# A scan and a mixture of adapters on one core: stores of four chunks, five transfers under way, new orders

## The chip, the cores and the metric

The kernel runs on one core of a Trainium2 chip. The metric is the device time of one execution in microseconds; where several runs are told of, it is their median.

## The reference

Two inputs `a` and `b` of shape (8, 6400, 128) in float32 go through a first-order recurrence along the sequence, and its output through a mixture of eight adapters of rank 16, of which each row uses its two best.

```python
for t in range(S):                      # S = 6400, h of shape (8, 128)
    h = a[:, t] * h + b[:, t]
    out[:, t] = h
x = out.reshape(51200, 128)
logits = x @ w_gate                     # (51200, 8)
topk = np.argpartition(-logits, 2, axis=1)[:, :2]
w = softmax of the two logits
delta[rows of expert e] += w * ((x @ A[e]) @ B[e])      # A: 128x16, B: 16x128
return x + delta
```

## The kernel before

The 51,200 rows are cut into 100 **chunks** of 512 rows, of four **blocks** of 128 rows each. A chunk goes through these steps, whose names are those of the orders below:

- `la`, `lb` (L396): SyncE loads `a` and `b` in tiles `a_tm` and `b_tm`, two chunks (512 KB) at a time; the first four chunks come singly, and ScalarE issues one of their loads. From chunk 4 on a partition takes eight rows, 4 KB, that follow each other in memory. There are `NL` = 6 places for each input.
- `A`, `B`, `P` (L417): TensorE transposes `a` into `pA` and `b` into `pB`; `P` holds `b` of a chunk and `a` of the next, woven. `fi` (L446) are transposes to fill time.
- `ae` (L435): ScalarE copies `pA` to `a_st`.
- `sc` (L482): VectorE runs the scan along 512 columns and writes `xT` in float16. Every 6,400 rows it starts anew, which makes two scans of a chunk in some cases. `xT` holds `NX` = 24 chunks.
- `Z` (L500), `ze` (L506): TensorE multiplies a unit of mostly six blocks of x with the adapters' down-projection and the gate's weights; ScalarE copies the result to `zl`, which holds `NZ` = 120 blocks.
- `g1` to `g8`, `gx`, `w1`: the gate's weights for a group of up to four units, on VectorE and GpSimd, with a sigmoid (`w1`) on ScalarE.
- `mu` (L569): GpSimd, sometimes VectorE, multiplies `zl` with the weights to `zw`.
- `T` (L578), `te` (L300): transposes of `zw` and their copy to `zwT`, by VectorE or ScalarE.
- `D` (L588, L589): for each block the product with the identity brings x back, and the one with `B` adds the delta, in `pO`.
- `oe` (L300): a copy to `outt`, mostly by ScalarE. It holds `NO` = 72 blocks, 18 chunks.
- `st` (L631): SyncE stores finished chunks, 48 times two chunks and 4 times one. A store's chunks lie in one **tile** of x in which a partition holds rows that follow each other in memory (8 rows, 4 KB, for two chunks). `Z` picks its blocks across that tile, so it waits for the scan of the tile's last chunk. The store of chunks 68 and 69 goes in two DMAs, of 124 and of 4 partitions (`SPLIT`).

Each engine executes its instructions in an order that is written out in `ORDER`. Each step lists the steps that it depends on, and `waits()` makes of these the semaphore waits, leaving out those that another wait implies. A load waits for the transposes of what stood in its place before; a store waits for the copies of its chunks; a copy to `outt` waits for the store of what stood there. An engine that waits holds up everything behind it in its order; SyncE issues loads and stores in one order. At the end SyncE waits for the landing of the stores.

Of the kernel before, what the change touches and what calls it, by code (L numbers as in the profile page):

```python
# [9 lines left out]

UNITS = [4] * 3 + [6] * 62 + [4] * 4
GROUPS = [1, 2] + [4] * 15 + [2, 1, 1, 1, 1]
STORES = [2] * 48 + [1] * 4
SPLIT = {68: [124, 4]}
TOP8 = 4
WARM = 16
FILL = {k: 4 for k in range(7, 15)}
HEAD = 4
NL = 6
NA = 3  # L20
NX = 24
NZ = 120
NO = 72
NW = 4
NG = 8
NS = 16
TAIL_CHUNKS = 12
ORDER = {
# [16 lines left out]
    ),  # L45
    "act": (
# [16 lines left out]
    ),  # L63
    "dve": (
# [14 lines left out]
    ),  # L79
    "pool": (  # L80
# [8 lines left out]
    ),  # L89
# [9 lines left out]
    ),  # L99
}  # L100

# [26 lines left out]
        assert len(named) == len(self.ops)  # L128
        self.order = {e: [named[name] for name in ORDER[e].split()] for e in self.ENGINES}
        assert sum(len(o) for o in self.order.values()) == len(self.ops)  # L130
        for e in self.ENGINES:
            n = 0
            for op in self.order[e]:
# [597 lines left out]
```

## Time and profile before

| | |
|---|---|
| median of three runs | 201.57 us (201.27 to 201.87) |
| profiled execution | 201.01 us |
| its span, first to last instruction | 199.2 us |
| busy: PE, DVE, ACT, POOL | 185.2, 175.0, 176.9, 136.0 us |
| moved by DMA | 79.26 MB, mean 398 GB/s |
| granted TensorE clock | 0.994 |

PE is TensorE's matmul, PEld its weight load, DVE VectorE, ACT ScalarE, POOL GpSimd, SP SyncE. A `q` behind an engine's name is its sequencer, which issues DMAs and waits. L396 is line 396 of the kernel. The DMA share is the mean busy share of the core's sixteen DMA engines; it can go above 1 because packets overlap on an engine. "To landing" is the time from a DMA's issue until its semaphore tells of its end. Durations come from the one profiled execution.

### The profile page before, as it was taken

How to read it: one execution, taken by the hardware profiler on the slowest of the kernel's cores; microseconds unless marked ns; L12 is line 12 of the kernel's file. 1: busy time of each engine (PE TensorE's matmuls, PEld its weight loads, DVE VectorE, ACT ScalarE, POOL GpSimd, SP SyncE). 2: the span in 40 equal slices, each digit the busy share in tenths (PEclk: the TensorE clock that was granted, in tenths of full speed). 3: DMA queues.
4: the chain of work that ended last, by engine and by line, in shares of the span. 5: the costliest groups of instructions: out<-in, count | busy, mean ns of one | idle time of the engine just before them, and what ended most of it. 6: DMA issues, size and time to landing. Idle time of an engine off the chain costs nothing.

```text
span 199.2 us, 7709 instructions
## 1 busy us (share of the span) xinstructions
PE 185.2 (93%) x3224; PEld 165.5 (83%) x3224; DVE 175.0 (88%) x291; ACT 176.9 (89%) x327; POOL 136.0 (68%) x168
## 2 busy tenths in 40 slices
PE   6899999999998979999999999999999999999990
PEld 6778888889987968899989989889988978878970
DVE  1599999989999879799999999999999899899980
ACT  2378699999988979899999999999999989999981
POOL 3210186878786657969989998796598978676520
PEclk9999999999999999999999999999999999999997
DMA  5999999999999999999999999999999999999796
GB/s 214 385 414 406 410 407 407 409 406 410 411 410 413 414 411 412 415 414 408 414 415 406 411 410 416 411 411 415 414 412 414 417 410 412 406 393 392 298 405 254
DMA packets 22921, 79.26 MB, mean 398 GB/s; under 512 B 2664, under 2 KB 2920, under 8 KB 22888
## 3 DMA queue, kind: packets, MB, share of 16 engines
q1 hardware_dynamic: 22312, 78.39, 98.1%
q8 instruction: 25, 0.41, 0.8%
q10 hardware_dynamic: 576, 0.40, 0.6%
q14 instruction: 8, 0.07, 0.1%
HBM read 52.56 MB, written 26.21 MB: 395 GB/s over the span
## 4 chain that ended last, share of the span: by engine, by line
PE 80%; ACT 5%; DMA 4%; issue 3%; SPq 2%; POOL 2%; DVE 1%; DVEq 0%
PE pB L417 23%; PE pO L588 13%; PE pZ L500 13%; PE pO L578 12%; PE pO L589 10%; PE pA L417 5%; DMA a_tm<-in_a_dram 4%; ACT outt L300 3%; PE pA L446 2%; SPq L396 2%; POOL zw L569 2%; ACT zwT L300 1%; ACT a_st L435 1%; ACT zl L506 1%; DVE xT L482 1%
## 5 line engine op out<-in xcount | busy, mean ns | idle before, releaser
L482 DVE TENSOR_TENSOR_SCAN xT<-a_st,xT,pB 128x512 f16<-128x512 f32 x96 | 120.4, 1254 | 6.6 <-PE pA L417 3.1
L569 POOL TENSOR_TENSOR zw<-zl,g 128x512 f16<-128x512 f32 x90 | 94.5, 1065 | 29.2 <-DVE g L554 23.2
L417 PE MATMUL pB<-ident_f,b_tm 64*128 64x64 f32 (+1 forms) x784 | 67.5, 229 | 1.2 <-issue 0.5
L417 PE MATMUL pA<-ident_f,a_tm 64*128 64x64 f32 (+1 forms) x784 | 67.8, 229 | 0.6 <-issue 0.4
L435 ACT COPY a_st<-pA 128x512 f32<-128x512 f32 x100 | 59.0, 613 | 7.9 <-PE pA L417 7.2
L417 PEld LDWEIGHTS pB<-ident_f,b_tm 64*128 64x128 f32 (+1 forms) x784 | 55.8, 139 | 10.9 <-issue 3.4
L506 ACT COPY zl<-pZ 128x816 f32<-128x816 f32 (+1 forms) x69 | 58.1, 842 | 1.7 <-PE pZ L500 1.6
L588 PE MATMUL pO<-ident_h,xT 128*128 128x128 f16 x368 | 55.2, 233 | 2.0 <-issue 1.8
L417 PEld LDWEIGHTS pA<-ident_f,a_tm 64*128 64x128 f32 (+1 forms) x784 | 56.0, 139 | 1.2 <-DMA a_tm<-in_a_dram 0.7
L300 ACT COPY outt<-pO 128x512 f32<-128x512 f32 x87 | 52.2, 609 | 4.6 <-PE pO L589 4.1
L589 PE MATMUL pO<-cst_h,zwT 128*128 128x128 f16 x368 | 53.0, 219 | 1.7 <-issue 1.7
L588 PEld LDWEIGHTS pO<-ident_h,xT 128*128 128x128 f16 x368 | 46.3, 144 | 4.9 <-issue 2.1
L589 PEld LDWEIGHTS pO<-cst_h,zwT 128*128 128x128 f16 x368 | 39.6, 108 | 1.8 <-issue 1.8
L500 PE MATMUL pZ<-cst_h,xT 128*128 128x136 f16 x400 | 37.8, 229 | 0.5 <-issue 0.4
L578 PE MATMUL pO<-ident_h,zw 128*128 128x128 f16 x368 | 35.5, 220 | 1.1 <-POOL zw L569 0.4
L500 PEld LDWEIGHTS pZ<-cst_h,xT 128*128 128x128 f16 x400 | 30.6, 145 | 1.5 <-DVE cst_h L324 0.2
L578 PEld LDWEIGHTS pO<-ident_h,zw 128*128 128x128 f16 x368 | 22.3, 97 | 5.5 <-POOL zw L569 1.3
L300 DVE COPY zwT<-pO 128x512 f16<-128x512 f16 x56 | 23.0, 414 | 3.5 <-PE pO L578 3.1
L300 ACT COPY zwT<-pO 128x512 f16<-128x512 f16 x36 | 21.4, 600 | 0.9 <-PE pO L578 0.8
L545 POOL TENSOR_TENSOR L<-L,k 128x192 f32<-128x192 f32 x14 | 8.8, 631 | 4.6 <-DVE L L543 4.0
L482 DVE TENSOR_TENSOR_SCAN xT<-a_st,pB 128x512 f16<-128x512 f32 (+1 forms) x8 | 7.5, 938 | 4.5 <-PE pB L417 4.4
L548 POOL TENSOR_TENSOR k<-k,L 128x192 f32<-128x192 f32 (+1 forms) x17 | 9.1, 535 | 2.5 <-DVE L L539 1.8
(56 smaller groups left out, 120.0 us busy)
## 6 DMA issues: line engine op xcount, KB each, us to landing
a_tm<-in_a_dram SPq DMA_DIRECT2D x48, 512.0 KB, 13.3
b_tm<-in_b_dram SPq DMA_DIRECT2D x48, 512.0 KB, 13.4
out_dram<-outt SPq DMA_DIRECT2D x47, 512.0 KB, 11.9
a_tm<-in_a_dram SPq DMA_DIRECT2D x4, 256.0 KB, 4.9
out_dram<-outt SPq DMA_DIRECT2D x4, 256.0 KB, 4.0
b_tm<-in_b_dram SPq DMA_DIRECT2D x3, 256.0 KB, 5.6
out_dram<-outt SPq DMA_DIRECT2D x1, 496.0 KB
b_tm<-in_b_dram ACTq DMA_DIRECT2D x1, 256.0 KB, 4.0
```

Source lines behind the costliest of these rows:

```text
L300: return e.copy(dst, src) if e is eng["act"] else e.tensor_copy(dst, src)
L417: last = e.transpose(*args)
L435: lambda e: e.copy(a_st[c % NA][:, :], pA[:, c % 2, :]))
L482: last = e.tensor_tensor_scan(out=x[:, s0:s1], data0=a_st[c % NA][:, s0:s1], data1=pB[:, c % 2, s0:s1], initial=init, op0=ALU.mult, op1=AL ...
L500: last = e.matmul(pZ[:, k // (n // 2), o : o + W], xblock(b0 + k), Awg_h)
L506: lambda e: e.copy(zl[:, zb : zb + n, :].rearrange("p (h k) w -> p h (k w)", h=2), pZ[:, :, 0 : n // 2 * W]))
L545: d3 = wide(5, [d3], lambda e: e.tensor_tensor(out=ll, in0=ll, in1=kk, op=ALU.add))
L548: d6 = wide(7, [d2, d5], lambda e: e.tensor_tensor(out=kk, in0=kk, in1=ll, op=ALU.add))
L569: lambda e: e.tensor_tensor(out=wv, in0=zv, in1=gv, op=ALU.mult))
L578: last = e.transpose(ptile[:, k * 128 : k * 128 + 128], zz[:, k, :], ident_h[:, :])
L588: e.matmul(dst, xblock(b0 + k), ident_h[:, :], start=True, stop=False)
L589: last = e.matmul(dst, zt[:, k * 128 : k * 128 + 128], B_h, start=False, stop=True)
```

## The change

- Stores take four chunks: two stores of two chunks, 23 of four, four of one. A partition's rows of a four-chunk store lie in one stretch of 8 KB. The tiles of x follow, so that `Z` waits for the scan of the last of four chunks.
- Four stores, those from chunk 20, 44, 68 and 84, go in five DMAs each, of 112, 4, 4, 4 and 4 partitions; the one split of before is gone.
- On SyncE each transfer also waits until the fifth before it in the order has landed. A store in parts counts as one.
- Five places for loads (6), 32 chunks of `xT` (24), 96 blocks of `zl` (120), 96 blocks of `outt` (72).
- New orders on all engines. The engine of some steps changes: 92 output copies are on ScalarE (95) and 8 on VectorE (5); 40 copies to `zwT` are on ScalarE (38) and 60 on VectorE (62); 11 `mu` on VectorE (10); among the gate's steps some go from one of VectorE and GpSimd to the other.

```diff
-STORES = [2] * 48 + [1] * 4
-SPLIT = {68: [124, 4]}
+STORES = [2,2]+[4]*23+[1]*4
+SPLIT = {c:[112,4,4,4,4] for c in (20,44,68,84)}
...
-NL = 6
+NL = 5
 NA = 3
-NX = 24
-NZ = 120
-NO = 72
+NX = 32
+NZ = 96
+NO = 96
...
+AHEAD = 5
 ORDER = {
     "pe": (
...
     "sp": (
-        "la0 lb1 la1 la3 lb2 la2 lb3 la4 lb4 la6 lb6 la8 lb8 la10 lb10 la12 lb12 la14 lb14 la16 lb16 la18 lb20 lb18 "
-        "la20 la24 la22 st0 lb22 la26 lb24 lb26 la28 la30 lb30 st2 lb28 lb34 la32 la34 lb32 lb36 la36 st6 st4 lb38 "
...
-        "st60 la98 st62 st72 st64 lb98 st66 st68 st78 st76 st70 st74 st82 st80 st86 st84 st90 st88 st92 st94 st96 "
-        "st97 st98 st99 "
+        "la0 la1 la2 lb1 la3 lb2 la4 lb3 lb4 la6 lb6 la8 lb8 la10 lb10 la12 lb12 lb14 la14 la16 lb18 lb16 la18 la20 "
+        "lb20 lb24 la22 st0 lb22 la24 la28 la26 lb26 lb28 st2 lb30 la30 la32 lb34 la36 lb32 la34 la38 lb36 st8 lb38 "
+        "la40 lb40 st12 la42 lb42 lb46 la44 lb44 lb48 la46 la48 st4 la50 lb52 lb50 la54 la52 st20 la56 lb54 la60 lb56 "
...
+        "lb92 la94 st52 lb94 la96 lb96 lb98 la98 st56 st60 st64 st76 st72 st68 st80 st84 st88 st92 st96 st97 st99 "
+        "st98 "
     ),
 }
...
         assert sum(len(o) for o in self.order.values()) == len(self.ops)
+        for before, op in zip(self.order["sp"], self.order["sp"][AHEAD:]):
+            op.deps = op.deps + [before]
```

More of the change, by code (lines that the diff above doesn't have):

```diff
@@ L12 @@
 GROUPS = [1, 2] + [4] * 15 + [2, 1, 1, 1, 1]
-STORES = [2] * 48 + [1] * 4
-SPLIT = {68: [124, 4]}
+STORES = [2,2]+[4]*23+[1]*4
+SPLIT = {c:[112,4,4,4,4] for c in (20,44,68,84)}
 TOP8 = 4
 WARM = 16
-FILL = {k: 4 for k in range(7, 15)}
+FILL = {k:4 for k in range(7,15)}
 HEAD = 4
-NL = 6
+NL = 5
 NA = 3
-NX = 24
-NZ = 120
-NO = 72
+NX = 32
+NZ = 96
+NO = 96
 NW = 4
```

111 rows, old and new, of the table ORDER are left out of this document.

## The prediction, made before the changed kernel ran

> **What bounds the kernel now.** I began with the slices of the page, because the change is about transfers, and then its queues and landing times.
>
> ```profile
> span 199.2 us, 7709 instructions
> PE 185.2 (93%) x3224; PEld 165.5 (83%) x3224; DVE 175.0 (88%) x291; ACT 176.9 (89%) x327; POOL 136.0 (68%) x168
> ...
> DMA  5999999999999999999999999999999999999796
> ...
> DMA packets 22921, 79.26 MB, mean 398 GB/s; under 512 B 2664, under 2 KB 2920, under 8 KB 22888
> ...
> q1 hardware_dynamic: 22312, 78.39, 98.1%
> q8 instruction: 25, 0.41, 0.8%
> ...
> a_tm<-in_a_dram SPq DMA_DIRECT2D x48, 512.0 KB, 13.3
> ...
> out_dram<-outt SPq DMA_DIRECT2D x47, 512.0 KB, 11.9
> ```
>
> The DMA digits are 9 from the second slice to the 37th. SyncE's queue q1 carries 78.39 MB and fills 98.1% of sixteen engines' span. A load of 512 KB lands 13.3 us after its issue. The next view cuts the span into stretches; its columns are busy time by engine with instruction counts, granted clock, DMA share, GB/s.
>
> ```profile
> 30.00:60.00 30.00, 28.64 (x543) 25.83 (x543) 28.32 (x37) 29.04 (x53) 23.71 (x28) 1.00 1.03 410
> 60.00:90.00 30.00, 27.49 (x510) 24.75 (x508) 26.22 (x40) 27.04 (x51) 21.64 (x26) 1.00 1.03 413
> 90.00:120.00 30.00, 29.85 (x560) 27.25 (x559) 29.15 (x40) 29.71 (x56) 27.85 (x35) 1.00 1.02 411
> 120.00:150.00 30.00, 29.48 (x554) 26.88 (x553) 28.57 (x44) 29.27 (x54) 23.45 (x28) 1.00 1.03 413
> 150.00:182.00 32.00, 30.39 (x526) 26.48 (x524) 29.44 (x55) 30.39 (x58) 25.97 (x29) 1.00 1.01 408
> 182.00:188.00 6.00, 5.93 (x96) 5.64 (x95) 6.00 (x24) 6.00 (x15) 2.59 (x4) 1.00 0.78 312
> 188.00:196.00 8.00, 5.96 (x89) 5.04 (x86) 5.10 (x23) 6.14 (x14) 2.12 (x3) 1.00 1.01 398
> ```
>
> The share is at or above 1.01 in every stretch from 30 to 182 us, at 408 to 413 GB/s. No engine is free either: ACT is busy for 29.7 of 30 us in one stretch. So two paces have to be compared. A chunk moves 256 KB of a, of b and of output, 786 KB, which at 412 GB/s is **1.91 us of transfers a chunk**. For the other pace I took the scans alone, stretch by stretch (busy time of DVE with the count, clock, share, GB/s):
>
> ```profile
> 30.00:60.00 30.00, 23.82 (x19) 1.00 1.03 410
> 60.00:90.00 30.00, 20.00 (x18) 1.00 1.03 413
> 90.00:120.00 30.00, 23.41 (x20) 1.00 1.02 411
> 120.00:150.00 30.00, 21.26 (x18) 1.00 1.03 413
> 150.00:180.00 30.00, 17.28 (x15) 1.00 1.02 408
> ```
>
> Between 30 and 150 us 75 scans run, some five of them second halves of a chunk where a batch begins: 70 chunks in 120 us, **1.71 us of computing a chunk**. From 150 to 180 there are 15 scans in 30 us, 2 us each. The engines run faster than the transfers for as long as loads issued ahead and free output places allow, and then fall back to the transfers' pace. The chain of waits on the page shows the opposite, 80% PE; but it follows the last releaser, and PE is kept supplied as long as loads are issued ahead of stores. The end confirms it:
>
> ```profile
> L396 SPq DMA_DIRECT2D b_tm<-in_b_dram x1: 445/445/445, 164.8 to 164.8; - x1
> ...
> DMA to landing us min/median/max: 13.3/13.3/13.3
> ```
>
> The last load is issued at 164.8 and lands at 178.1. In SyncE's order 33 stores of two chunks stand ahead of it, so 34 chunks, 8.9 MB, follow; at 412 GB/s that is 21.6 us, and the span ends 21.1 us later. The transfers are the bound to the last microsecond, and the sum is made on them.
>
> **The change part by part.**
>
> *Rows of 8 KB.* 23 stores of four chunks take the place of 46 stores of two. Their 92 chunks are 5,888 packets of 4 KB now and 2,944 of 8 KB then; bytes stay. Counted with their parts, 53 store transfers become 45, at 16 completion packets each: 128 fewer. Together 3,072 packets go from q1. What a packet costs beside its bytes comes from two pairs of windows of the DMA view, of which each pair differs in the mean size:
>
> ```profile
> q1 hardware_dynamic: 4499, 16.39, 101.5%
> ...
> q1 hardware_dynamic: 1116, 2.98, 82.7%
> ...
> q1 hardware_dynamic: 695, 1.26, 88.7%
> ...
> q1 hardware_dynamic: 685, 2.49, 103.1%
> ```
>
> The first is 60 to 100 us: 1.015 x 16 engines x 40 us = 649.6 us for 4,499 packets and 16.39 MB. The second is 190 to 199.2 us: 121.7 us for 1,116 packets and 2.98 MB. Solved for a price per packet and one per MB they give **12 ns a packet** and 36.3 us a MB. The third and fourth, 4 to 8 us and 10 to 16 us, give 19 ns in the same way, but there the constants' small packets share the engines. I take 12, since that pair holds stores. The saving is 3,072 x 12 ns / 16 engines = **2.3 us**; 19 ns would make it 3.6, and a price of nothing 0. A loss is bounded by the one row with packets of 16 KB: q8's 25 take 0.8% of 3,187 us, 1.02 us each, 62 us a MB. I give that no weight for the size, because such a packet takes turns with q1's on its engine, which the share above 1 shows.
>
> The Trainium skill, "DMA: Bandwidth & Descriptors", section "Why small descriptors are slow", speaks for less: a fixed three cycles or so a packet, which at the 850 MHz of its bandwidth section is an estimated 3.5 ns. By it the saving would be 0.7 us, and the total about 201.5. The rows above say 12 to 19 ns, and I go by them.
>
> *Four stores in five parts.* Today one store goes in parts of 124 and 4 partitions; afterwards four go in 112, 4, 4, 4, 4. Their bytes are the same. SyncE issues 16 more DMAs, at 0.45 us (the row of the last load) 7 us of its time, beside waits of 78 us below. I cost it at 0, with both signs open. If small parts use fewer engines than a full one, those fall behind by twelve 8 KB rows in all, 12 x 310 ns = 3.7 us, unless they were ahead; today's 124-part, in rows of 4 KB, would do the like.
>
> *Five under way.* Each transfer on SyncE now also waits until the fifth before it has landed. Behind such a wait stands everything later on SyncE, loads and stores; PE, and through it ACT and DVE, wait for the loads.
>
> ```profile
> SPq L396 <- PE pA L417: 36.1, 26, 4.3
> SPq L631 <- ACT outt L300: 23.3, 13, 5.0
> ...
> SPq L631 <- ACT sd L549: 12.9, 4, 8.8
> SPq L670 <- DVE outt L300: 5.8, 1, 5.8
> ...
> DMA to landing us min/median/max: 3.1/3.9/4.3
> ```
>
> Of these the last row is of the loads issued in the first 2 us, 256 KB each: 3.1 us for one that finds nothing ahead. At 1.27 us for 512 KB, today's 13.3 us are ten transfers deep; afterwards there are five, 6.4 us. When one lands, four are left, 5.1 us of work, and the next one's first byte needs some 3.1 - 0.6 = 2.5 us, so nothing runs dry unless SyncE then stands for over 2.6 us. Today it stands up to 4.3, 5.0, 5.8 and 8.8 us. But it will reach each transfer later, by up to 13.3 - 6.4 = 6.9 us, in which the engines move on; one load place less (two chunks, 3.8 us) takes part of that back, and 3.1 us are left. All but the 8.8 then fall near or below 2.6. At the start the first five are issued by 3 us, and the sixth waits for the first, landed at 3.8 to 4 us, while four of 256 KB are still to come. I cost the gate at 0; without that cover it is 4 us, below.
>
> *More output places, and the orders.* 72 blocks become 96, xT goes from 24 chunks to 32, zl from 120 blocks to 96. In the new order 15 stores (56 chunks) precede the last load, now 33 (66 chunks): it lands 2.6 MB / 412 = 6.4 us earlier, and 1.2 us more by packets already saved, near 170.5. The transfers' total is not changed by that, but it gives the engines room at the end:
>
> ```profile
> 193.67 1.17 ACT L300 COPY outt<-pB 128x512 f32<-128x512 f32 x2 [0.23 <-PE pB L589]
> ...
> L300 ACT COPY outt<-pO 128x512 f32<-128x512 f32 x87 | 52.2, 609 | 4.6 <-PE pO L589 4.1
> ```
>
> Today the last copy ends at 194.8, 16.7 us after the last load. From 170.5 that gives 187.2, where stores would still have some 9 us to go. ACT does three output copies fewer, DVE three more, and two zwT copies go from DVE to ACT; both engines' sums move by under 2 us. Z of a unit now waits for the scan of the last of four chunks, not of two; PE's order still places another P and further steps between that P and the Z.
>
> *The coarse end.* A four-chunk store can't start before its fourth copy; the last of them waits two copies longer than one of two chunks, 2 x 0.61 = 1.2 us, or 0 if the queue holds work then. I take half, **0.6 us**.
>
> **Sum.** 199.2 - 2.3 + 0.6 = 197.5 us of span. With the 1.8 us around it (the profiled execution took 201.01 us) that is 199.3, and since the median of the runs, 201.57, is 0.56 above that execution, **199.8 us**.
>
> **The rivals.**
>
> *The gate starves the engines (slower).* Its place is SyncE's wait ahead of a load that is drawn forward (la60 goes before la58, lb46 before la44) and whose place must first be emptied. It decides once SyncE stands for more than 2.6 us with four under way. With 3.1 us gained, the two longest waits of today would leave 8.8 - 3.1 - 2.6 = 3.1 us and 5.8 - 3.1 - 2.6 = 0.1 us; if the later arrival gains only 2.7, 3.5 and 0.5, so 4 us: 199.8 + 4 = **203.8 us**. For it: the transfers have no slack, every idle microsecond of theirs is one of the total. Against it: the load waits, 36.1 us in 26 cases, are short (mean 1.4).
>
> *A row's size is worth nothing.* If the bytes alone set a packet's time, only the 0.6 us stays: 202.2, or 201.6 if the queue hides that too; **201.8 us**. Against it are both pairs of windows. The skill's three cycles belong here.
>
> *The engines become the bound.* With all five busy, the new orders may cost the engines their 0.2 us a chunk of lead. At 1.91 us a chunk nothing would be gained; 0.02 us a chunk worse is 2 us: **203.5 us**. Against it stand 75 scans in 120 us.
>
> *The end gains too.* From 182 to 188 us the share is 0.78: 0.23 x 6 = 1.4 us of idle engines because stores were not ready. If the earlier last load closes that, **198.4 us**.
>
> **How the numbers follow.** Forecast 0.50, end gains too 0.11, row size worthless 0.13, gate starves 0.18, engines bound 0.08. About 0.3%, 0.6 us, is what a measurement of this kernel can tell from no change. Faster: 0.50 + 0.11 = 0.61, and 0.01 of the worthless-rows case; within 0.3%: the rest of that, 0.12; slower: 0.26. The range goes from 198.2, the end's gain with a little of a 19 ns packet, to 202.8, half of the gate's price and the worthless rows; beyond it lie most of the gate's and half of the engines' case, under 2 in 10.
>
> **What would show it.** q1 should have some 3,070 packets fewer at 78.4 MB; the share should stay at or above 1.0 from 10 us on past 180; loads should land some 6 to 7 us after issue; the last load should land near 171. If the share sags below 0.95 in a middle stretch while SyncE waits for PE, the gate was mispriced. If the share holds and the GB/s don't rise above 412, the row size was. If PE, DVE or ACT runs on to within 4 us of the end with the last stores landing at once, the engines are the bound.

## The result, and the profile after

The changed kernel takes **208.18 us** (median of four runs, 207.12 to 212.88), the kernel before 201.42 us: a ratio of 1.0316, 95% interval 1.0248 to 1.0383. Runs more than 1.5% above the fastest of their kernel count in the medians given here but not in the ratios: it is the one of 212.88 us here, and one of four in the experiments without the gate, with parts of 16, with parts for the early stores and with the last split store whole. The forecast was 199.8 us with a range to 202.8. The kernel is 6.4 us slower where 1.8 us of gain were expected.

The page of the kernel after, with the rows that answer to those of before:

```profile
span 205.4 us, 7749 instructions
...
PE 185.8 (90%) x3224; PEld 165.4 (81%) x3224; DVE 176.1 (86%) x289; ACT 177.8 (87%) x327; POOL 135.0 (66%) x171
...
DMA  6999999999999999989999999999999999999796
GB/s 221 383 413 407 404 409 285 411 397 374 408 397 409 391 401 416 416 310 359 402 415 405 416 412 406 413 420 397 415 406 387 415 410 414 427 412 369 249 380 260
DMA packets 19682, 79.27 MB, mean 386 GB/s; under 512 B 2368, under 2 KB 2624, under 8 KB 16704
...
q1 hardware_dynamic: 19072, 78.39, 97.2%
...
a_tm<-in_a_dram SPq DMA_DIRECT2D x48, 512.0 KB, 6.7
b_tm<-in_b_dram SPq DMA_DIRECT2D x48, 512.0 KB, 7.4
```

The engines do the same work: PE 185.8 us for 185.2, ACT 177.8 for 176.9. The bytes of q1 are the same, its packets are 3,240 fewer (3,070 were expected), and loads land 6.7 and 7.4 us after issue, as expected of five under way. But the mean pace fell from 398 to 386 GB/s. The DMA digits hardly show it: below 9 stand only an 8 in the eighteenth slice, where before there was a 9, and the 7 in the thirty-eighth, which was there before. The GB/s row shows three holes: the seventh slice (285), the eighteenth and nineteenth (310, 359), and the thirty-eighth (249). By stretches (busy time by engine with counts, granted clock, DMA share, GB/s), the kernel after:

```profile
30.00:60.00 30.00, 28.28 (x528) 25.13 (x526) 27.66 (x35) 28.72 (x54) 21.46 (x26) 1.00 1.01 380
60.00:90.00 30.00, 29.59 (x562) 27.02 (x561) 28.63 (x43) 29.46 (x55) 23.26 (x30) 1.00 1.00 397
90.00:120.00 30.00, 27.35 (x512) 24.45 (x510) 26.80 (x38) 27.81 (x51) 23.88 (x28) 1.00 1.01 393
120.00:150.00 30.00, 29.90 (x561) 27.30 (x560) 28.46 (x46) 28.68 (x54) 26.27 (x33) 1.00 1.02 411
150.00:182.00 32.00, 29.80 (x522) 26.35 (x516) 28.18 (x46) 28.95 (x53) 24.48 (x30) 1.00 1.01 410
182.00:190.00 8.00, 7.75 (x111) 6.75 (x111) 7.94 (x28) 7.88 (x18) 4.16 (x4) 1.00 1.02 382
190.00:199.00 9.00, 6.97 (x102) 5.80 (x100) 6.75 (x26) 6.95 (x16) 2.57 (x6) 1.00 0.82 300
199.00:205.40 6.40, 0.00 (x0) 0.00 (x0) 0.00 (x0) 0.00 (x0) 0.00 (x0) 0.54 0.74 291
```

From 30 to 120 us the share is 1.00 to 1.01 where the kernel before has 1.02 to 1.03, and the pace is 380 to 397 GB/s where that one has 410 to 413. The share counts the time that packets take, however slowly they go: it fell by 1 to 3%, the pace by 4 to 7%. From 190 us on both fall. SyncE's waits in the kernel after (total, times, longest):

```profile
SPq L397 <- DMA b_tm<-in_b_dram: 33.6, 39, 1.9
SPq L397 <- DMA a_tm<-in_a_dram: 32.9, 37, 1.9
SPq L671 <- DMA out_dram<-outt: 16.3, 10, 2.2
...
SPq L671 <- PE pA L418: 3.2, 3, 2.6
...
SPq L397 <- PE pA L418: 0.7, 1, 0.7
```

SyncE now waits for its own transfers to land; the waits for PE's `pA`, 36.1 us before, have shrunk to the 3.2 and 0.7 us of the last two rows.

### The profile page after: what moved, and what is told of

Its sections match the earlier page's. It is cut to its first block, busy times and chain, and to the rows that moved or that the text cites. A ratio compares the mean times of both kernels' runs of the same rounds, so it can differ in the third digit from the quotient of the medians.

```text
span 205.4 us, 7749 instructions
## 1 busy us (share of the span) xinstructions
PE 185.8 (90%) x3224; PEld 165.4 (81%) x3224; DVE 176.1 (86%) x289; ACT 177.8 (87%) x327; POOL 135.0 (66%) x171
## 3 DMA queue, kind: packets, MB, share of 16 engines
q1 hardware_dynamic: 19072, 78.39, 97.2%
## 4 chain that ended last, share of the span: by engine, by line
DMA 57%; PE 29%; ACT 7%; DVE 1%; SPq 1%; issue 1%
DMA b_tm<-in_b_dram 37%; DMA a_tm<-in_a_dram 12%; PE pB L418 9%; DMA out_dram<-outt 8%; PE pO L589 5%; PE pO L579 5%; PE pZ L501 4%; PE pO L590 3%; ACT outt L301 3%; PE pA L418 1%; ACT zwT L301 1%; ACT zl L507 1%; SPq L397 1%; PE pA L447 1%; ACT a_st L436 1%
## 5 line engine op out<-in xcount | busy, mean ns | idle before, releaser
L570 POOL TENSOR_TENSOR zw<-zl,g 128x512 f16<-128x512 f32 x89 | 92.7, 1061 | 23.6 <-DVE g L555 22.0
L418 PE MATMUL pB<-ident_f,b_tm 64*128 64x64 f32 (+1 forms) x784 | 68.6, 229 | 7.5 <-DMA b_tm<-in_b_dram 5.4
L418 PE MATMUL pA<-ident_f,a_tm 64*128 64x64 f32 (+1 forms) x784 | 68.7, 230 | 0.1
L301 ACT COPY outt<-pO 128x512 f32<-128x512 f32 x85 | 51.3, 611 | 3.6 <-PE pO L590 2.4
L579 PE MATMUL pO<-ident_h,zw 128*128 128x128 f16 x368 | 34.9, 220 | 0.8 <-DVE outt L301 0.4
L301 ACT COPY zwT<-pO 128x512 f16<-128x512 f16 x37 | 22.0, 602 | 1.3 <-PE pO L579 0.8
L546 POOL TENSOR_TENSOR L<-L,k 128x192 f32<-128x192 f32 (+1 forms) x16 | 9.3, 582 | 10.0 <-DVE L L544 9.6
L549 POOL TENSOR_TENSOR k<-k,L 128x192 f32<-128x192 f32 (+2 forms) x19 | 10.4, 549 | 4.5 <-DVE k L539 2.7
L548 POOL TENSOR_TENSOR L<-k,m 128x192 f32<-128x192 f32 (+1 forms) x14 | 7.4, 530 | 7.0 <-DVE m L547 6.9
```

The costliest lines, as they stand in the source:

```text
L301: return e.copy(dst, src) if e is eng["act"] else e.tensor_copy(dst, src)
L418: last = e.transpose(*args)
L546: d3 = wide(5, [d3], lambda e: e.tensor_tensor(out=ll, in0=ll, in1=kk, op=ALU.add))
L549: d6 = wide(7, [d2, d5], lambda e: e.tensor_tensor(out=kk, in0=kk, in1=ll, op=ALU.add))
L570: lambda e: e.tensor_tensor(out=wv, in0=zv, in1=gv, op=ALU.mult))
L579: last = e.transpose(ptile[:, k * 128 : k * 128 + 128], zz[:, k, :], ident_h[:, :])
```

## The experiments

Ratios are to the kernel before on the same chip, with 95% intervals; 1% is 2.0 us. A difference of two ratios has the interval of both, taken as independent.

**One part taken out at a time.** *Without the gate:*

```diff
-        for before, op in zip(self.order["sp"], self.order["sp"][AHEAD:]):
-            op.deps = op.deps + [before]
```

> The changed kernel without the rule that five transfers are under way; all else stays, the parts too. Theory 'gate' (a queue of five lets the sixteen DMA engines run dry at SyncE's waits and takes from the faster engines the lead with which they cover their own delays; it costs most of the 6.7 us): 201 to 203 us, loads landing 12 us or more after issue instead of 7. Theory 'parts' (the 4-partition transfers hold SyncE up; a deep queue covers that only in part): 204 to 207 us. Theory 'orders' (the new orders and the coarse stores are slower by themselves): 206 us or more.

Measured: 207.31 us, 1.0256 (1.0190 to 1.0322).

*Without the parts:*

```diff
-SPLIT = {c:[112,4,4,4,4] for c in (20,44,68,84)}
+SPLIT = {}
```

> The changed kernel with all stores sent whole, the gate of five kept. Theory 'gate': 206 to 208 us, since nothing of the queue's depth changes. Theory 'parts': 203 to 205 us, and the stretches after 83 us and after 177 us, where SyncE takes 1 to 2.5 us for the issue of a small part, lose their dips in GB/s. Theory 'orders': unchanged within 1 us.

Measured: 204.76 us, 1.0159 (1.0112 to 1.0206).

*Without both:*

> The changed kernel with neither the gate nor the parts: new orders, four-chunk stores in 8 KB rows and the new places alone. If gate and parts are all that is slow, 199 to 202 us, the forecast of 199.8 among them if the longer rows are worth their 2 us, 201.5 if they are worth nothing. Theory 'orders': 204 us or more.

Measured: 203.06 us, 1.0094 (1.0061 to 1.0127).

So the parts cost 1.6% (±0.8), with the gate (1.0316 against 1.0159) and without it (1.0256 against 1.0094): **3.2 us**, the largest term. The gate costs 0.65% (±0.6) without the parts and 0.6% (±0.9) with them: **1.3 us**, not far from what these runs can tell from nothing. Orders, stores and places together cost 0.9% (±0.3), 1.9 us. All three are on the slow side; no single one is the cause.

**The gate alone, and how deep.** The kernel before with the gate of five:

```diff
+        for before, op in zip(self.order["sp"], self.order["sp"][5:]):
+            op.deps = op.deps + [before]
```

> The kernel before with the gate of five as the only edit. Theory 'gate': 203 to 208 us, slower by 2 us or more. Theory 'parts' or 'orders': 201 to 202 us, since a queue of five transfers holds 6.4 us of work. Its order was made without the gate and has its stores as wide as loads, so a loss here may be larger or smaller than in the changed kernel.

Measured: 206.70 us, 1.0263 (1.0206 to 1.0321). The same gate costs 5.3 us (±1.2) here, against 1.3 us (±1.1) in the changed kernel. No run isolates why it is dearer here; the stores of this kernel are half as large, so that five transfers hold fewer bytes. With eleven in place of five:

> The kernel before with a gate of eleven transfers in place of none (that of five cost it 5.3 us). If the price of a gate is that few transfers under way leave some of the sixteen engines without work, it falls with the number: today's loads land 13.3 us after issue, which is ten to eleven transfers, so 201.2 to 202.2 us. If the price is that of one more wait for each transfer, it stays near 206 us.

Measured: 201.88 us, 1.0002 (0.9972 to 1.0032). The wait itself costs nothing that can be measured; the small number does. And five, but only from the eighteenth transfer on (`sp[12:]` and `sp[17:]`):

> The kernel before with the gate of five from the eighteenth transfer on, so that the loads of the first 10 us are issued as before. If the gate's 5.3 us arise at the start (the transfers then move 384 to 392 GB/s until 40 us, where the kernel before moves 406 to 416), most of them go: 201.5 to 203 us. If it is that the sixteen engines can no longer run ahead of one another anywhere, most stay: 204.5 to 206.5 us.

Measured: 204.66 us, 1.0148 (1.0077 to 1.0220). So 3.0 us (±1.5) arise later and the rest at the start, 1.15% (±0.9) or 2.3 us. The rows agree. First the kernel before, then with the gate of five, then with the late gate, last with the gate of eleven:

```profile
8.00:16.00 8.00, 7.28 (x90) 5.61 (x91) 6.84 (x12) 4.80 (x11) 0.51 (x2) 1.00 1.03 416
16.00:30.00 14.00, 14.00 (x238) 12.11 (x236) 13.44 (x23) 11.65 (x21) 5.43 (x8) 1.00 1.02 406
30.00:40.00 10.00, 9.51 (x175) 8.41 (x174) 9.54 (x12) 9.88 (x18) 7.73 (x10) 1.00 1.03 409
170.00:182.00 12.00, 11.41 (x178) 9.59 (x175) 11.11 (x28) 11.50 (x23) 9.11 (x9) 1.00 1.00 398
```

```profile
8.00:16.00 8.00, 6.28 (x70) 4.70 (x68) 6.03 (x11) 4.52 (x9) 0.51 (x2) 0.93 0.99 384
16.00:30.00 14.00, 14.00 (x222) 12.13 (x222) 12.18 (x20) 9.97 (x19) 4.32 (x6) 0.92 1.01 392
30.00:40.00 10.00, 9.87 (x183) 8.54 (x182) 9.46 (x12) 10.00 (x19) 7.54 (x10) 1.00 1.01 383
```

```profile
8.00:16.00 8.00, 7.28 (x97) 5.84 (x95) 7.39 (x14) 5.02 (x12) 0.51 (x2) 1.00 1.03 415
60.00:90.00 30.00, 29.66 (x555) 27.03 (x552) 28.35 (x42) 29.61 (x55) 25.00 (x31) 1.00 1.01 400
170.00:182.00 12.00, 11.38 (x176) 9.51 (x175) 11.12 (x30) 11.51 (x22) 8.81 (x9) 1.00 0.97 365
```

```profile
8.00:16.00 8.00, 7.33 (x97) 5.77 (x95) 7.36 (x14) 5.03 (x12) 0.51 (x2) 1.00 1.03 415
```

With the gate from the start, 8 to 40 us lose 32 x 8 + 14 x 14 + 26 x 10 = 712 GB/s times us, 0.71 MB, 1.7 us at 410. With the late gate the early stretch is as before (415), and 60 to 90 and 170 to 182 us lose 0.39 and 0.40 MB, 1.9 us. The granted TensorE clock is lower with the early gate (0.93 and 0.92), but SyncE waits for PE for only 2.6 us in that whole run, so it isn't a slower PE that holds the transfers up. That the sixteen DMA engines hinder one another when the slowest decides on the next transfer is the explanation I hold; no view shows the engines one by one, so it is argued, not shown. It covers at most a part: from 8 to 16 us the share fell by 4% (1.03 to 0.99) and the pace by 8% (416 to 384), so packets also took longer for their bytes, and why is open.

**What the parts cost, and where.** Parts of 16 partitions in place of 4:

```diff
-SPLIT = {c:[112,4,4,4,4] for c in (20,44,68,84)}
+SPLIT = {c:[64,16,16,16,16] for c in (20,44,68,84)}
```

> The changed kernel, with the four split stores sent as 64, 16, 16, 16 and 16 partitions in place of 112, 4, 4, 4 and 4. As many DMAs, as many rows; every part can spread over sixteen engines. If the price of the parts (3.4 us, 208.2 against 204.8 without them) is that of more DMAs on SyncE or of more of them to complete, it stays: 207 to 209 us, with SyncE again some 5 us on one split store. If it is that a part of four partitions can only go to four engines, which fall behind or whose queues make SyncE wait, it goes: 204 to 205.5 us.

Measured: 207.69 us, 1.0269 (1.0209 to 1.0328). Most of it stays, 1.1% (±0.8) above no parts, so the size of a part is not the main cause. That it is the number of DMAs, five in place of one, is what is left, and it is argued: no run sends two or three. Then parts for fewer of the stores, `(20,44)` and `(20,44,68)`:

> The changed kernel with the first two of its split stores (from chunks 20 and 44) in parts, the last two (68 and 84) whole. If each split store costs alike, half of the 3.4 us goes: 206.5 us. If the price arises where nothing follows that could make up for it, at the end, nearly all of it goes: 205 us. If it is the middle ones, after each of which five transfers under way run dry, nearly all stays: 207.5 us or more.

> The changed kernel with the last of its four split stores (from chunk 84) sent whole, the others in parts. If the price (3.4 to 3.8 us, all in the stores from 68 and 84) comes from SyncE standing 7 us on the parts of the store from 84 while the ones behind it are ready, it goes: 204 to 205.3 us. If the store from 68, on whose parts SyncE stands 7 us as well, has its share, half stays: 206 to 206.8 us.

Measured: 204.36 us, 1.0122 (1.0082 to 1.0163), and 204.99 us, 1.0150 (1.0087 to 1.0213). Both intervals hold the 1.0159 of no parts at all. Within what can be measured the whole price is that of **the one store from chunk 84**; no run has that store alone in parts. SyncE's stores in the kernel after (start, length, count), and the duration of one issue in ns (minimum, median, maximum) at two of these places:

```profile
83.43 5.17 SPq L632 DMA_DIRECT2D out_dram<-outt  x5
...
145.96 1.79 SPq L632 DMA_DIRECT2D out_dram<-outt  x5
...
187.69 6.97 SPq L632 DMA_DIRECT2D out_dram<-outt  x5
```

```profile
L632 SPq DMA_DIRECT2D out_dram<-outt x5: 309/319/344, 146.0 to 147.4; - x5
...
L632 SPq DMA_DIRECT2D out_dram<-outt x5: 322/1536/1992, 187.7 to 193.6; - x5
```

Five parts take SyncE 1.8 us at 146, but 5.2 at 83 and 7.0 at 188, and in that time it does nothing else. Why an issue is long at some times is open: neither the size of a part (16 partitions cost nearly as much as 4) nor a wait that the profile lists explains it. At 83 us the loads behind it are late and the pace falls to 310 and 359 (the slices above), but by the run with parts at 20 and 44 alone, and by the one with the last store whole, such a hole is made up later. At 188 us only stores are left behind it: the next two go out at 194.8 and 195.2 us, with no wait of SyncE's between. The kernel after, and with the last split store whole:

```profile
182.00:190.00 8.00, 7.75 (x111) 6.75 (x111) 7.94 (x28) 7.88 (x18) 4.16 (x4) 1.00 1.02 382
190.00:196.00 6.00, 5.30 (x82) 4.64 (x80) 5.73 (x24) 5.09 (x13) 2.57 (x6) 1.00 0.74 251
```

```profile
182.00:190.00 8.00, 7.87 (x121) 7.16 (x120) 8.00 (x30) 7.67 (x18) 3.31 (x5) 1.00 1.00 378
190.00:196.00 6.00, 4.24 (x58) 3.16 (x56) 4.10 (x17) 4.03 (x10) 1.50 (x5) 1.00 0.99 412
```

The share goes from 0.74 to 0.99: 161 GB/s x 6 us = 0.97 MB, 2.4 us of the 3.2. But one profile of each can't divide the price between single issues. Up to this store the two programs are the same, and yet the five parts of the store from chunk 68 took 1.0 to 1.1 us each in the kernel after, while in the other run the last four took 0.3 to 0.4, and its store from chunk 84 was issued 2.8 us earlier. It is the times of the runs that place the price.

**The load drawn forward.** What is left without gate and parts has one hole, at 30 to 40 us. SyncE's order there has `lb24` ahead of `la22` and `lb22`:

```diff
-lb20 lb24 la22 st0 lb22 la24
+lb20 la22 st0 lb22 lb24 la24
```

> The kernel without gate and parts (203.1 us), with one load moved in SyncE's order: lb24, which now stands two places ahead of its turn and waits there for the transposes of chunk 14 and 15 with the loads of chunks 22 behind it, goes behind lb22. If its wait, after which the transfers moved 359 GB/s from 30 to 40 us where the kernel before moves 409, makes up what is left of the loss, the dip closes and 1.2 us (0.5 MB at 410 GB/s) go: 201.6 to 202.2 us. If the engines are late there for other reasons, the wait moves to the next load and the time stays within 202.7 to 203.5 us.

Measured: 202.03 us, 1.0022 (0.9989 to 1.0055). SyncE's waits from 20 to 36 us and the stretch, first of the kernel without gate and parts, then with `lb24` in its turn:

```profile
SPq L395 <- PE pA L416: 12.0, 5, 6.3
...
30.00:40.00 10.00, 9.86 (x187) 8.71 (x187) 9.72 (x11) 10.00 (x19) 7.41 (x9) 1.00 1.01 359
```

```profile
SPq L395 <- PE pA L416: 8.9, 6, 4.0
SPq L630 <- ACT outt L299: 4.7, 1, 4.7
...
30.00:40.00 10.00, 9.87 (x188) 8.79 (x187) 9.73 (x12) 10.00 (x20) 7.29 (x8) 1.00 1.03 408
```

SyncE waits no less in this stretch: in place of 6.3 us ahead of `lb24`, with two loads of chunk 22 behind it, it waits 4.7 us ahead of `st0`, when `la22` is already issued. The pace goes from 359 to 408, and 0.7% (±0.5), **1.5 us**, go from the time. In the hole the share still says 1.01.

**The size of a row.** A first look, in the kernel without gate and parts: each store of four chunks as two DMAs of 4 KB rows.

```diff
-return [e.dma_start(dst[p : p + n], view[p : p + n]) for p, n in zip(lows, cuts)]
+return [e.dma_start(dst[:, i * J * m // h : (i + 1) * J * m // h], view[:, i * J * m // h : (i + 1) * J * m // h])
+        for i in range(h)]          # h = 2: rows of 4 KB; h = 4: rows of 2 KB
```

> The kernel without the gate and without parts (203.1 us), with each store of four chunks sent as two DMAs whose rows are 4 KB, at the same place of SyncE's order: the tiles, the orders and the places stay. 2,944 packets more. By the prediction's 12 ns a packet it is 2.2 us slower, 205.3 us. If a row's size is worth nothing, it takes 202.7 to 203.5 us; as the first half of each store can land earlier it could even gain a little.

Measured: 203.92 us, 1.0128 (1.0066 to 1.0189), 0.3% (±0.7) more than with whole stores: nothing and 2 us are both within it. Again with `lb24` in its turn, with rows of 4 KB and of 2 KB and more runs:

> The kernel without gate and parts and with lb24 in its turn (202.0 us), each store of four chunks sent as two DMAs with rows of 4 KB. 2,944 packets and 23 DMAs more. By the prediction's 12 ns a packet 2.2 us slower: 204.2 us. If a row's size is worth nothing: 201.7 to 202.5 us.

> The same with four DMAs a store and rows of 2 KB: 8,832 packets and 69 DMAs more than with rows of 8 KB. At 12 ns a packet 6.6 us slower: 208.6 us. If a row's size is worth nothing and SyncE has time for the DMAs: 201.7 to 203 us. If 2 KB rows cost but 4 KB ones don't, there is a size above which it no longer counts.

Measured: 203.06 us, 1.0074 (1.0053 to 1.0095), and 209.19 us, 1.0362 (1.0322 to 1.0402). The queue and two stretches with rows of 8, 4 and 2 KB:

```profile
q1 hardware_dynamic: 19008, 78.39, 97.4%
...
120.00:150.00 30.00, 30.00 (x567) 27.54 (x565) 29.26 (x46) 28.80 (x55) 25.78 (x31) 1.00 1.02 415
150.00:182.00 32.00, 31.31 (x529) 27.69 (x526) 29.78 (x58) 30.49 (x59) 24.38 (x29) 1.00 1.02 417
```

```profile
q1 hardware_dynamic: 22320, 78.39, 97.8%
...
120.00:150.00 30.00, 29.30 (x549) 26.70 (x549) 28.61 (x45) 28.03 (x53) 24.82 (x30) 1.00 1.03 413
150.00:182.00 32.00, 31.25 (x534) 27.54 (x530) 29.64 (x58) 30.42 (x57) 25.33 (x30) 1.00 1.03 413
```

```profile
q1 hardware_dynamic: 29232, 78.39, 98.0%
...
150.00:182.00 32.00, 30.75 (x536) 27.27 (x536) 28.97 (x49) 29.82 (x56) 25.30 (x30) 1.00 1.03 402
```

From 8 to 4 KB: 0.52% or 1.05 us for 3,312 packets on sixteen engines, **5 ns a packet** (1.3 to 8.9 by the intervals, if those are taken as independent). It shows as 417 against 413 GB/s. SyncE also has 23 more DMAs to issue with rows of 4 KB, and whatever they cost is in the 5 ns. From 4 to 2 KB it is 5.8 us for 6,912 packets, 13 ns, and 48 more DMAs (the two stores of two chunks go in two as well); the two aren't told apart.

**Splits elsewhere.** The kernel before without its one split:

```diff
-SPLIT = {68: [124, 4]}
+SPLIT = {}
```

> The kernel before, with its one split store (124 and 4 partitions, chunk 68) sent whole. If unequal parts put rows on few engines, it gains up to 1 to 3 us, since the 124 partitions come near the end, where little time is left to make up for it: 198.5 to 200.5 us. If only the number of DMAs costs, one less is worth 0.3 us at most: 201.0 to 201.6 us. If the split store was put there because some engines lead, it is slower: over 202 us.

Measured: 202.27 us, 1.0029 (1.0010 to 1.0048): that split is worth 0.6 us (±0.4), and the changed kernel gave it up. The kernel with `lb24` in its turn, with early parts and with that split:

> The kernel without gate and with lb24 in its turn, with the stores from chunks 20 and 44 in the changed kernel's five parts. If parts cost only where SyncE has no time left, at the end, it takes 201.5 to 202.5 us, as without them. If each split store costs alike, 1.7 to 2 us more: 203.8 us.

> The kernel without gate and with lb24 in its turn, with the store from chunk 68 in the two parts of the kernel before, 124 and 4 partitions. Taking that split out of the kernel before made it 0.3% slower. If it does the same good here: 201.3 to 201.7 us. If it does nothing, 202.0; if two parts of rows of 8 KB cost SyncE or four engines time near the end, 203 us or more.

Measured: 201.52 us, 1.0011 (0.9982 to 1.0041), and 210.33 us, 1.0423 (1.0386 to 1.0460). Early parts cost nothing that can be measured. The split into 124 and 4, good for 0.6 us in the kernel before, with its stores of 512 KB in rows of 4 KB, costs 8 us with stores of 1 MB in rows of 8 KB. Its DMA view from 165 to 195 us, in 40 slices:

```profile
DMA  9999999999999999999999987999967989852222
GB/s 393 421 415 437 410 448 421 421 415 393 459 393 437 415 426 437 415 360 360 382 382 360 350 317 306 306 328 317 295 186 240 339 306 339 273 142 76 98 109 98
```

The last slices have a share of 0.2 to 0.3 at 76 to 109 GB/s, a quarter of sixteen engines' pace: four of them work on. That fits 124 partitions spread over four engines, 31 rows of 8 KB each. The time is lost because the copies of the last chunks wait for the places of this store:

```profile
ACT outt L299 <- DMA out_dram<-outt: 7.5, 1, 7.5
```

The packet counts of q1 fit as well. Sixteen more DMAs of 4 partitions add 64 packets (19,072 for the kernel after, 19,008 without parts), four each; sixteen more of 16 partitions add 256 (19,264), sixteen each; and the two parts of 124 and 4 have 8 packets fewer than one whole store (19,000), which is four each in place of sixteen. The Trainium skill, "DMA: Bandwidth & Descriptors", section "Why a DMA increments its semaphore by 16 and not by 1", states the rule: the largest number up to 16 that divides the partitions, so 4 for 124 and for 4, and 16 for 112. These slices, at a quarter of the pace, and these counts agree.

**The coarse end.** The last two stores of four chunks made four of two, and the last four made eight:

```diff
-STORES = [2,2]+[4]*23+[1]*4
+STORES = [2,2]+[4]*21+[2]*4+[1]*4
```

> The kernel without gate, with lb24 in its turn and parts at chunks 20 and 44 alone (201.5 us), with the last two stores of four chunks (from 88 and 92) made four of two. From 182 to 196 us its transfers move 397 to 398 GB/s, where 410 is the pace: 0.2 MB, 0.4 us. If the coarse end costs what the forecast gave it, 0.6 us go: 200.8 to 201.2 us. If other waits hold the last stores, 201.4 to 201.9 us.

> The same with the last four stores of four chunks (from 80 on) made eight of two. By the coarse end 200.6 to 201.2 us. If the four more transfers on SyncE or the smaller rows (512 packets more, 0.2 us at what the runs with 4 KB rows give) take back what the end gains, 201.4 to 202 us.

Measured: 201.56 us, 1.0005 (0.9977 to 1.0033), and 201.69 us, 1.0015 (0.9992 to 1.0038). Nothing is gained beside 1.0011: the coarse end costs nothing that can be measured. No version here beats the kernel before; four without gate and with `lb24` in its turn reach it.

## Why the prediction was wrong, by its own steps

- **The bound** was right. The terms found show as lost transfer pace, while PE, DVE and ACT did the same work. One count under it is off: in the order of the kernel before, 34 stores and not 33 stand ahead of the last load, so 32 chunks follow, 8.4 MB or 20.4 us, beside the 21.1 us to the end. The sum doesn't use it.
- **Parts, costed at 0:** the step that failed most; they cost 3.2 us. The prediction counted 16 DMAs at 0.45 us beside SyncE's 78 us of waits. The 0.45 was one issue at another moment; in the end phase an issue took up to 2 us, and the waits in the middle are no cover for the time after 182 us. The other thing it left open, that engines with small parts fall behind, was not most of it for parts of four, since parts of 16 cost nearly as much; but it is what a part of 124 does. Why an issue gets long stays open.
- **The gate, costed at 0:** 1.3 us in this kernel and 5.3 us in the one before. The step "when one lands, four are left, 5.1 us of work" expected the full pace with four or five under way, and the runs show 384 to 392 GB/s in place of 406 to 416 at the start; by the explanation argued above, sixteen engines are not one queue. The start, worked out to the sixth issue and then put at nothing, alone costs 2.3 us (±1.8) on the kernel before. The rival named SyncE's waits for a place to be emptied. Those waits shrank; the waits for landings cost.
- **Rows of 8 KB, -2.3 us:** about -1.05, the issues of 23 DMAs included. The 12 ns came from two windows that differ in more than the packet's mean size, the second of them at the end where the share is 0.83, and from shares, of which one of 1.01 stands here for 359 GB/s as well as for 410. The estimate by the Trainium skill, "DMA: Bandwidth & Descriptors", section "Why small descriptors are slow", was 3.5 ns a packet; the measured 5 ns with its interval holds that and excludes 12.
- **The coarse end, +0.6:** nothing measurable.
- **The orders, at nothing:** one load drawn forward cost 1.5 us with five places. The prediction saw that kind of wait (lb46 before la44) as the gate's place; it costs without any gate, and at chunk 24. The split that was given up was worth 0.6 us in the kernel before. The count of packets was off as well: a part of four partitions has four packets for its end, not 16, so 3,240 went in place of 3,072.
- **The last load** was put near 171 with no gain from it. In the kernel after it is issued at 168.9 and lands 6.3 us later, the shortest of the last three:

```profile
L397 SPq DMA_DIRECT2D a_tm<-in_a_dram x1: 328/328/328, 168.9 to 168.9; - x1
...
DMA to landing us min/median/max: 6.3/8.8/8.8
```

That is 175.2, 3 us before the kernel before, and the end still came 6.2 us later, since stores were held up after it.

By ratios the loss adds up, as one part was taken out after the other: parts 1.57, gate 0.65, `lb24` 0.72, and 0.22% for the rest, 3.16% in all. In that rest the rows' gain of 0.5% and the lost split's 0.3% (if it is worth as much here as in the kernel before) leave some 0.4%, 0.9 us, that no run isolates; places and the other orders are in it.

The prediction's sign for a mispriced row, "the share holds and the GB/s don't rise above 412", came true in the changed kernel for other reasons: without gate and parts and with `lb24` in its turn the pace did rise, to 415 and 417 from 120 us on.

## What to carry to other kernels

Where transfers are the bound, read GB/s and not the share: the share was 1.01 in a hole of 359 GB/s, and still 0.89 in the eighteenth slice of the kernel after, at 310, where 410 is the pace. A DMA's issue belongs to the stretch in which it is made, so extra issues and drawn-forward loads are costed at that place with what is queued behind them, not against the engine's idle time over the span. A limit on transfers under way has a price that depends on its depth: of the two depths tried on the kernel before, whose loads land after ten transfers' time, five cost 5.3 us and eleven nothing that can be measured.

## What was not expected of the hardware

- An issue of one store DMA on SyncE took 0.32 us at 146 us and up to 2.0 us at 188 us, in the same kernel and with the same partitions; a kernel with parts of 16 partitions takes 207.69 us, with parts of 4 208.18. Why an issue is long is open.
- A DMA of 124 partitions runs at about a quarter of the pace, 76 to 109 GB/s, to its end, at a share of 0.2 to 0.3.
- With a gate of five the pace from 8 to 16 us falls from 416 to 384 GB/s at a DMA share of 0.99, and with eleven it is 415; the granted TensorE clock, 1.00 before, is 0.93 and 0.92 from 8 to 30 us with that gate.
